# Weights requested ahead of K and V and used two heads later, a first MLP layer in single-column steps, and the last dx sums moved to the end

## The chip, the cores and the metric

The kernel runs on one core of a Trainium2 chip. The metric is the device time of one execution in microseconds (us), median of several runs. TensorE is called PE, VectorE DVE, ScalarE ACT, GpSimd POOL and SyncE SP. In this kernel SP issues all loads, in program order, and POOL issues all large stores.

## The reference, cut to what matters

One decoding step of a gated mix of attention and an MLP, forward and backward. There are 32 heads; each has a K and a V cache of 4096 x 128 in bf16 (1 MiB each), which must be read once, and gradients dK and dV of the same size, which must be written once.

```python
def _A_ref(x, k_cache, v_cache, wq, wo):          # x: [1, 1, 640]
    q = (x @ wq).reshape(B, Sq, H, Dh).transpose(0, 2, 1, 3)
    scores = jnp.einsum("bhqd,bhkd->bhqk", q, k_cache) * (Dh ** -0.5)
    p = _softmax(scores, axis=-1)
    o = jnp.einsum("bhqk,bhkd->bhqd", p, v_cache)
    return o.transpose(0, 2, 1, 3).reshape(B, Sq, H * Dh) @ wo
def _B_ref(x, w1, b1, w2):                        # F = 1728
    h = x @ w1 + b1
    return (h * tanh(softplus(h))) @ w2
# out = g * a + (1 - g) * b;  g = sigmoid(sum(x * gate_w))
# returned: out, and the gradients of x, k_cache, v_cache, wq, wo, w1, b1, w2, gate_w
```

K, V, wq, wo, w1 and w2 are 82 MB to read; their gradients are 82 MB to write. The arithmetic is that of one query row, so the work is a copy with some matrix-vector products on the way.

## The kernel before

Heads come in groups of four. One pass of `period(h)` handles a head: transposes of V on PE, softmax, dP, dV, dQ, and, for head h+1, the transposes of K and the scores. K and V of head h+3 are requested when head h starts (four buffers each). A group needs weights: a wo tile (640 KB, three buffers) and half of a wq tile (1280 KB, two buffers).

```python
def load_k(h):                                   # load_v, load_wq, load_wo and load_w2 alike, all on SP
    if h < H:
        kts[h] = kv_in.tile([P, J, Dh], BF16, name="Kn", tag="Kn", bufs=KB)   # KB = 4
        nc.sync.dma_start(kts[h][:], Kv[h])
```

Everything that is not a head's own work is cut into steps. A step has a kind (P for PE, D for DVE, T for a trifle) and names the steps that must be done in an earlier slot. `slot` is called three times in a head; it runs what is ready, up to p steps of kind P and d of kind D.

```python
def slot(h, p=2, d=1):
    slot_no[0] += 1
    room = {"P": p, "D": d, "T": 99}
    for kind in ("T", "D", "P"):
        for st in list(steps):
            name, k, fn, deps, head = st
            if k != kind or head > h or not room[k]:
                continue
            if all(done.get(x, 1 << 30) < slot_no[0] for x in deps):
                fn(); done[name] = slot_no[0]; steps.remove(st); room[k] -= 1
```

`prep_steps(g)` prepares a group: `qcol` (20 matmuls of x with wq), `doa` and `dob` (DVE sums over wo), and broadcasts of both. `finish_steps(g)` makes dwo in place of wo and stores it, and, for a whole wq tile, five dx sums. `mlp_steps()` is the MLP:

```python
def h_part(a, b):                                # first layer, columns a to b of 18
    def f():
        hps["t"] = gr_ps.tile([FP, FCN], F32, name="h_ps", tag="gr")
        for fc in range(a, b):
            for rc in range(RC):                 # RC = 5 matmuls a column
                nc.tensor.matmul(hps["t"][:, fc:fc + 1],
                                 lhsT=w1_sb[:, rc, :].rearrange("p (q c) -> p q c", c=FCN)[:, :, fc],
                                 rhs=x_bf[:, rc:rc + 1], start=(rc == 0), stop=(rc == RC - 1))
    return f
# ...
for k in range(0, FCN, 3):
    add(f"h{k}", "P", h_part(k, k + 3), (f"hadd{k - 3}",) if k else (), H0)
    add(f"hadd{k}", "T", h_add(k, k + 3), (f"h{k}",), H0)
# ... w2 comes in three chunks with two buffers: b{c} and dh{c}_{i} read chunk c,
#     dw2 overwrites it and stores it, and then chunk 2 is loaded into the buffer of chunk 0
        if c < 2:
            done[f"w2_{c}"] = -1
        else:
            add(f"w2_{c}", "T", lambda c=c: load_w2(c), (f"dw2_{c - 2}",), H0)
```

The loop over the heads and the end:

```python
for h in range(H):
    hh, g = h % G, h // G
    load_k(h + 3)
    load_v(h + 3)
    if hh == 0 and g + 1 < NG:                   # preparation of the next group goes first in the list
        rest = steps[:]; steps.clear(); prep_steps(g + 1, h); steps.extend(rest)
    if hh == 3:
        load_wo(g + 2)                           # (asserts cut)
        if g % 2 == 0:
            load_wq(g // 2 + 1)
    # ... (dwq blocks from head H - 3 on, cut)
    period(h)
    # ... (finish_steps(g) after the fourth head, cut)
dk_half(H - 1, 0); dk_half(H - 1, 1)
while steps:
    slot(H, 9, 9)                                # among these the five dx sums of the last wq tile
dwq_l = wts.tile([P, RC, GD], BF16, name="dwq_l", tag="wo_g", bufs=3)
for rc in range(RC):
    nc.vector.tensor_scalar(dwq_l[:, rc, :], dq_bc[:, CL:], x_f[:, rc:rc + 1], None, ALU.mult)
nc.gpsimd.dma_start(dwq_v[:, :, CL:], dwq_l[:])
# ... (out, dx and dgate_w from small columns: three small stores)
```

## Time and profile before

| | before |
|---|---|
| time, median of 3 runs | 441.23 us (440.04 to 445.35) |
| span of the profiled execution | 440.2 us |
| moved by DMA | 165.06 MB, mean 375 GB/s |
| PE, DVE, ACT busy | 71%, 70%, 40% |

The first lines are from the profile's page of the kernel before. The rows of section 2 cut the span into 40 slices of 11 us: PEclk is the granted clock in tenths, DMA the busy share of the 16 DMA engines in tenths, GB/s what they moved.

```profile
span 440.2 us, 15621 instructions
...
PE 314.6 (71%) x6932; PEld 291.8 (66%) x6932; DVE 306.6 (70%) x782; ACT 174.8 (40%) x394; POOL 50.6 (11%) x92
...
PEclk9999688596899999879995899959989899999755
DMA  7999999986899999989999799999999999997994
GB/s 251 422 391 399 424 426 414 381 329 214 348 387 362 400 393 389 416 323 391 375 420 409 276 363 400 422 388 360 324 415 422 418 381 422 421 406 305 407 417 187
DMA packets 26336, 165.06 MB, mean 375 GB/s; under 512 B 2812, under 2 KB 2812, under 8 KB 10012
```

No engine is full, while many slices stand at 414 to 426 GB/s and others far below. At 422 GB/s the 165.06 MB take 391 us. This gives a useful measure: *lost capacity*. A window of 10 us at 234 GB/s has lost 10 x (422 - 234) / 422 = 4.5 us, and 391 us plus all such losses is the span.

The next lines are from the chain of waits of the kernel before (start, length, what): the chain of work that ended last, in order of time.

```profile
54.00 28.07 DMA wq_g<-in_A_wq_dram
82.11 0.69 PE qc_ps L258 x20
...
164.34 23.19 DMA wq_g<-in_A_wq_dram
...
215.21 24.09 DMA wo_g<-in_A_wo_dram
```

The `qcol` step of a group, and the DVE sums, wait for weights that were requested just before, behind two more MB of K and V. The windows of the kernel before show what such a wait does. The columns are stretch, length, busy us (and instructions) of PE, PEld, DVE, ACT and POOL, granted clock, DMA share, GB/s.

```profile
90.00:100.00 10.00, 9.06 (x172) 8.51 (x170) 6.25 (x17) 4.79 (x10) 0.53 (x1) 1.00 0.76 306
100.00:110.00 10.00, 9.35 (x134) 9.12 (x135) 4.26 (x12) 2.83 (x8) 1.07 (x2) 0.66 0.68 234
...
230.00:240.00 10.00, 0.00 (x0) 0.00 (x0) 0.68 (x1) 0.00 (x1) 0.00 (x0) 0.55 1.01 423
240.00:250.00 10.00, 8.28 (x156) 7.87 (x157) 9.45 (x25) 4.74 (x11) 0.53 (x1) 0.77 0.68 251
```

From 230 to 240 us PE did nothing and DMA was full, because it was still prefetching. The damage comes afterwards: the K and V buffers are full and no dK or dV is ready to be stored, so from 240 to 250 us DMA moves 251 GB/s. From 90 to 110 us there is a second pattern: PE is busy and yet DMA is starved. There the blocks of 15 first-layer matmuls lie, and the clock falls during some of them, not all (1.00 from 90 to 100 us). These are half-microsecond windows of the first such block, in the same columns:

```profile
45.00:45.50 0.50, 0.50 (x6) 0.50 (x4) 0.43 (x3) 0.00 (x0) 0.00 (x0) 1.00 1.12 475
47.00:47.50 0.50, 0.50 (x4) 0.50 (x5) 0.00 (x0) 0.00 (x0) 0.00 (x0) 0.50 1.01 426
```

Last, four waits of the kernel before (engine, line, what it waited for: us in total, times, longest): those of PE and DVE for weights, and two of SP's own. The first of SP's holds K and V back while a chunk of w2 waits for its buffer to be stored.

```profile
PE qc_ps L258 <- DMA wq_g<-in_A_wq_dram: 27.1, 4, 11.0
DVE junk L268 <- DMA wo_g<-in_A_wo_dram: 28.5, 6, 11.4
...
SPq L138 <- DMA out_dram<-w2c: 11.5, 1, 11.5
SPq L132 <- DMA out_dram<-wo_g: 3.4, 2, 2.5
```

### The profile page before, as it was taken

Reading aid. Unit: us, or ns where it says so; the run is one execution under the profiler, and the core shown is the slowest. Engines: PE = TensorE matmul, PEld = TensorE weight load, DVE = VectorE, ACT = ScalarE, POOL = GpSimd, SP = SyncE. Lnnn points to the kernel's source line nnn. Section 1 sums busy time; section 2 is a strip of 40 time slices with the busy share of each in tenths; the row PEclk is TensorE's granted clock in tenths of the full one; section 3 lists DMA queues with packets and bytes.
Section 4 is the critical chain, followed back from the end, with each engine's and each line's share of the span. In section 5 each row is a group of like instructions: output and inputs, shape, how many; then the busy total and the mean of one; then the engine's idle time right before and its main releaser. Section 6 shows DMA issues by size and latency. Waiting matters only on the chain.

```text
span 440.2 us, 15621 instructions
## 1 busy us (share of the span) xinstructions
PE 314.6 (71%) x6932; PEld 291.8 (66%) x6932; DVE 306.6 (70%) x782; ACT 174.8 (40%) x394; POOL 50.6 (11%) x92
## 2 busy tenths in 40 slices
PE   2688997598978788298870988439885988888310
PEld 2687997588877687187770878438784877778200
DVE  3385353544489888468962999447975999999980
ACT  2365242243345445154540555215643545546100
POOL 0001000000000100002100011000200011112520
PEclk9999688596899999879995899959989899999755
DMA  7999999986899999989999799999999999997994
GB/s 251 422 391 399 424 426 414 381 329 214 348 387 362 400 393 389 416 323 391 375 420 409 276 363 400 422 388 360 324 415 422 418 381 422 421 406 305 407 417 187
DMA packets 26336, 165.06 MB, mean 375 GB/s; under 512 B 2812, under 2 KB 2812, under 8 KB 10012
## 3 DMA queue, kind: packets, MB, share of 16 engines
q1 hardware_dynamic: 14156, 82.03, 48.1%
q0 software_dynamic: 12112, 82.03, 45.4%
q8 instruction: 54, 0.88, 0.8%
q14 instruction: 14, 0.11, 0.1%
HBM read 82.03 MB, written 82.03 MB: 373 GB/s over the span
## 4 chain that ended last, share of the span: by engine, by line
PE 28%; DVE 27%; DMA 25%; issue 10%; ACT 6%; POOL 1%; SPq 1%; ACTq 0%; POOLq 0%; DVEq 0%
DMA wq_g<-in_A_wq_dram 12%; DMA wo_g<-in_A_wo_dram 11%; PE tr L527 10%; DVE dK_sb L549 7%; ACT tT L529 6%; DVE dV_sb L549 5%; PE sA L535 4%; PE sB L646 4%; PE sA L593 3%; DVE junk L354 3%; DMA out_dram<-wo_g 3%; PE h_ps L383 2%; DVE junk L268 2%; DVE junk L484 1%; DVE dwq_t L665 1%
## 5 line engine op out<-in xcount | busy, mean ns | idle before, releaser
L529 ACT COPY tT<-tr 128x512 f32<-128x512 f32 x256 | 143.3, 588 | 170.1 <-PE tr L527 169.8
L535 PEld LDWEIGHTS <-tT 128*128 128x128 bf16 x2048 | 77.1, 98 | 39.7 <-ACT tT L529 29.9
L527 PE MATMUL tr<-ident_bf,Kn 128*128 128x128 bf16 x1024 | 84.9, 239 | 2.3 <-issue 2.3
L549 DVE TENSOR_TENSOR dV_sb<-p_bf,qd 128x2048 bf16<-128x2048 bf16 x64 | 78.0, 1219 | 0.2 <-issue 0.2
L549 DVE TENSOR_TENSOR dK_sb<-ds_bf,qd 128x2048 bf16<-128x2048 bf16 x64 | 77.7, 1216 | 0.0
L527 PE MATMUL tr<-ident_bf,Vn 128*128 128x128 bf16 x1024 | 74.7, 225 | 0.1
L527 PEld LDWEIGHTS <-Kn 128*128 128x128 bf16 x1024 | 72.0, 109 | 3.4 <-issue 2.7
L535 PE MATMUL sA<-qdc,tT 128*128 128x48 bf16 x1024 | 50.8, 190 | 26.2 <-ACT dq_all L651 15.2
L527 PEld LDWEIGHTS <-Vn 128*128 128x128 bf16 x1024 | 64.3, 101 | 0.7 <-issue 0.2
L268 DVE SCALAR_TENSOR_TENSOR junk<-wo_g,da_bc 128x640 bf16<-128x640 bf16 x32 | 26.3, 822 | 29.1 <-DMA wo_g<-in_A_wo_dram 28.5
L535 PE MATMUL sB<-qdc,tT 128*128 128x48 bf16 x1024 | 46.2, 183 | 0.0
L576 POOL DMA_DIRECT2D out_dram<-dV_sb x32 | 17.7, 553 | 196.2 <-DVE dV_sb L549 162.3
L646 PE MATMUL sB<-ds_bf,Kn 128*128 128x48 bf16 x1024 | 34.5, 189 | 3.3 <-issue 1.9
L593 PEld LDWEIGHTS <-Vn 128*128 128x128 bf16 x1024 | 30.5, 96 | 8.8 <-issue 8.5
L566 POOL DMA_DIRECT2D out_dram<-dK_sb x31 | 18.0, 580 | 153.5 <-DVE rz L615 73.9
L593 PE MATMUL sA<-e_bf,Vn 128*128 128x48 bf16 x1024 | 31.5, 183 | 5.6 <-DVE zs L613 1.6
L646 PEld LDWEIGHTS <-Kn 128*128 128x128 bf16 x1024 | 31.4, 100 | 3.8 <-issue 3.7
L597 DVE TENSOR_REDUCE m<-sA 128x1 f32<-128x32 f32 x32 | 6.1, 190 | 36.2 <-PE sA L535 36.1
L627 PE MATMUL sB<-ident_f,part 128*128 128x128 f32 x32 | 10.8, 339 | 19.8 <-DVE pj L624 19.6
L258 PE MATMUL qc_ps<-cols_bf,wq_g 128*128 128x1 bf16 x160 | 5.3, 165 | 27.1 <-DMA wq_g<-in_A_wq_dram 27.1
L354 DVE SCALAR_TENSOR_TENSOR junk<-wq_g,dq_bc 128x1024 bf16<-128x1024 bf16 x20 | 24.3, 1217 | 0.1
L633 DVE TENSOR_SCALAR_CACHE_REDUCE dj<-sB,rz 128x128 f32<-128x128 f32 x32 | 11.1, 346 | 18.6 <-PE sB L627 18.6
(137 smaller groups left out, 294.9 us busy)
## 6 DMA issues: line engine op xcount, KB each, us to landing
Kn<-in_A_k_cache_dram SPq DMA_DIRECT2D x32, 1024.0 KB, 8.6
Vn<-in_A_v_cache_dram SPq DMA_DIRECT2D x32, 1024.0 KB, 16.9
out_dram<-dV_sb POOLq DMA_DIRECT2D x32, 1024.0 KB, 9.2
out_dram<-dK_sb POOLq DMA_DIRECT2D x31, 1024.0 KB, 10.3
wq_g<-in_A_wq_dram SPq DMA_DIRECT2D x4, 1280.0 KB, 6.7
wo_g<-in_A_wo_dram SPq DMA_DIRECT2D x8, 640.0 KB, 16.5
out_dram<-wo_g POOLq DMA_DIRECT2D x8, 640.0 KB, 9.3
out_dram<-dwq_t POOLq DMA_DIRECT2D x5, 896.0 KB, 11.9
```

Of the source, the lines that this page charges most:

```text
L268: nc.vector.scalar_tensor_tensor(junk[:, 0:D], in0=wos[g][:, i, :], scalar=1.0, in1=da_bc[:], op0=ALU.mult, op1=ALU.mult, accum_out=gp["do ...
L354: nc.vector.scalar_tensor_tensor(junk[:], in0=wqs[w][:, rc, :], scalar=1.0, in1=dq_bc[:, w * WG * Dh:(w + 1) * WG * Dh], op0=ALU.mult, op1 ...
L527: nc.tensor.transpose(tp[:, t, :], src[:, c * 8 + t, :], ident_bf[:])
L529: nc.scalar.copy(f32v(sb[:].rearrange("p a b -> p (a b)")), f32v(tp[:].rearrange("p a b -> p (a b)")))
L535: nc.tensor.matmul(out[:, j:j + W], lhsT=tb[:, t, :], rhs=vec.to_broadcast([P, W]), start=True, stop=True)
L549: nc.vector.tensor_tensor(dst[:, a:b, :].rearrange("p j (a b) -> p j a b", b=2), col[:, a:b, :].unsqueeze(2).to_broadcast([P, n, Dh // 2, 2]),
L566: nc.gpsimd.dma_start(dKv[h], st["dK"][:])
L576: nc.gpsimd.dma_start(dVv[h], st["dV"][:])
L593: nc.tensor.matmul(O, lhsT=vts[h][:, j, :], rhs=st["e"][:, j:j + 1].to_broadcast([P, W]), start=(j == 0), stop=(j == J - 1))
L627: nc.tensor.transpose(PT, part[:].to_broadcast([P, P]), ident_f[:])
L633: nc.vector.tensor_scalar(dj[:], PT, rz[:], None, ALU.mult, ALU.add, accum_out=dd[:])
L646: nc.tensor.matmul(DQ, lhsT=kts[h][:, j, :], rhs=ds[:, j, 0:1].to_broadcast([P, W]), start=(j == 0), stop=(j == J - 1))
```

## The change

Its intent: let no head wait for weights, break up the long PE blocks, keep SP from waiting for the w2 store, and let the last large store leave before the last sums. The diff, with context cut:

```diff
         def h_part(a, b):
             def f():
-                hps["t"] = gr_ps.tile([FP, FCN], F32, name="h_ps", tag="gr")
+                hps[a] = gr_ps.tile([FP, FCN], F32, name="h_ps", tag="gr")
# ... (hps["t"] becomes hps[a] in h_part and h_add)
-        for k in range(0, FCN, 3):
-            add(f"h{k}", "P", h_part(k, k + 3), (f"hadd{k - 3}",) if k else (), H0)
-            add(f"hadd{k}", "T", h_add(k, k + 3), (f"h{k}",), H0)
-        add("act1", "D", act1, (f"hadd{FCN - 3}",), H0)
+        for k in range(FCN):
+            add(f"h{k}", "P", h_part(k, k + 1), (f"hadd{k - 2}",) if k > 1 else (), H0)
+            add(f"hadd{k}", "T", h_add(k, k + 1), (f"h{k}",), H0)
+        add("act1", "D", act1, (f"hadd{FCN - 1}",), H0)
# ...
-                add(f"w2_{c}", "T", lambda c=c: load_w2(c), (f"dw2_{c - 2}",), H0)
+                for k in range(4):
+                    add(f"w2w{k}_{c}", "T", lambda: None, (f"w2w{k - 1}_{c}" if k else f"dw2_{c - 2}",), H0)
+                add(f"w2_{c}", "T", lambda c=c: load_w2(c), (f"w2w3_{c}",), H0)
# ... (the last slot of a head)
-        slot(h)
+        slot(h, 2, 2)
# ... (the loop over heads; asserts cut)
+        if hh == 3:
+            load_wo(g + 2)
+            if g % 2 == 0:
+                load_wq(g // 2 + 1)
         load_k(h + 3)
         load_v(h + 3)
-        if hh == 0 and g + 1 < NG:
+        if hh == 1 and g + 1 < NG:
# ...
-        if hh == 3:
-            load_wo(g + 2)
-            if g % 2 == 0:
-                load_wq(g // 2 + 1)
# ... (the end)
+    last = [st for st in steps if st[0].startswith("dx")]
+    steps[:] = [st for st in steps if not st[0].startswith("dx")]
     while steps:
         slot(H, 9, 9)
# ... (dwq_l is made and stored)
+    steps.extend(last)
+    while steps:
+        slot(H, 9, 9)
```

More of the change, by code (lines that the diff above doesn't have):

```diff
@@ L379, in f @@
             def f():
-                hps["t"] = gr_ps.tile([FP, FCN], F32, name="h_ps", tag="gr")
+                hps[a] = gr_ps.tile([FP, FCN], F32, name="h_ps", tag="gr")
                 for fc in range(a, b):
                     for rc in range(RC):
-                        nc.tensor.matmul(hps["t"][:, fc:fc + 1],
+                        nc.tensor.matmul(hps[a][:, fc:fc + 1],
                                          lhsT=w1_sb[:, rc, :].rearrange("p (q c) -> p q c", c=FCN)[:, :, fc],
@@ L392, in f @@
                     m["h"] = T("h_sb")
-                nc.vector.tensor_tensor(m["h"][:, a:b], hps["t"][:, a:b], b1f[:, a:b], ALU.add)
+                nc.vector.tensor_tensor(m["h"][:, a:b], hps[a][:, a:b], b1f[:, a:b], ALU.add)
             return f
@@ L682 @@
         hh, g = h % G, h // G
+        if hh == 3:
+            assert g == 0 or f"dwo{g - 1}" in done
+            load_wo(g + 2)
+            if g % 2 == 0:
+                assert g == 0 or f"dx{RC - 1}_{g - 1}" in done
+                load_wq(g // 2 + 1)
         load_k(h + 3)
         load_v(h + 3)
-        if hh == 0 and g + 1 < NG:
+        if hh == 1 and g + 1 < NG:
             rest = steps[:]
@@ L689 @@
             steps.extend(rest)
-        if hh == 3:
-            assert g == 0 or f"dwo{g - 1}" in done
-            load_wo(g + 2)
-            if g % 2 == 0:
-                assert g == 0 or f"dx{RC - 1}_{g - 1}" in done or True
-                assert g == 0 or f"dx{g - 1}{RC - 1}_" in done or f"dx{RC - 1}_{g - 1}" in done
-                load_wq(g // 2 + 1)
         if h == H - 3:
```

## The prediction

> **What bounds it now.** The page: 165.06 MB of DMA in a 440.2 us span, 375 GB/s. In 10 us windows, undisturbed ones hold 418 to 427 GB/s (the Trainium skill, "Perfetto Trace Analysis", Roofline, gives a lone core's 16 engines about 435). At 422 the bytes alone need 391 us (my estimate). PE (71%) and DVE (70%) are not full; where nothing stalls, heads pass every 9.3 to 9.4 us (K load issues: 355.9, 365.3, 374.6), under the 12.2 us that a head's share of the bytes needs. So DMA should bound it; the 49 us above 391 are lost DMA capacity. From the windows: 4.5 us in the ramp, 6 in the tail, 38 between: about 10.5 from 80 to 120 us, 5 from 120 to 170, 5 from 190 to 220, 6 from 240 to 270, 5 from 290 to 320, 5 from 350 to 410.
>
> **Why it is lost.** (a) At a group's first head the matmuls for q, or the sums of do, wait for weights requested just before, behind that head's K and V. The chain of waits shows wq 28.1 us (54 to 82), 23.2 (164 to 188), wo 24.1 (215 to 239), 16.9 (322 to 339). PE idles some 8 to 12 us each time. DMA stays full then, prefetching, but afterwards no stores are ready and it sinks: 167 GB/s at 240-245, 274 at 190-195. (b) The MLP's first layer runs in blocks of 15 matmuls, 2.7 to 2.9 us; the granted clock falls to 0.50 during or after them for 3 to 7 us (46.5 to 53.5, 101 to 108). Heads 3 to 6 take 14 to 19 us. The skill ("TensorE: Matmul & The Clock Gate", Part 1) has the clock follow PE activity over windows of about 3.4 us; these spells fit. (c) SP waits 11.5 us for a w2c store, holding back K and V.
>
> **What the change does.** Weights go ahead of K and V and are used about two heads (20 us or more) later: (a) should vanish; K and V come up to 1.9 MB, 5 to 9 us, later, with two heads of them buffered. First-layer blocks become 5 matmuls, about 0.9 us, one per slot over heads 2 to 8; the clock should hold. The w2c reload waits four more slots, freeing SP; but its dh product comes one slot after the request, so DVE should stall there (head 15) some 5 to 10 us: a draw. A fourth DVE step per head ends the MLP at head 26, not 30. The last dx sums (5 x 1.24 us) move behind the last dwq store; DMA is full until 433 anyway: 0 to 1 us.
>
> **On the critical path:** the 38 us between ramp and tail; I expect 29 back: (a) 19, (b) 7, last heads 3. 391 + 4.5 + 6 + 9 = about 411 us.
>
> **What would show it.** PE's and DVE's waits on wq and wo (about 28 us each) fall under 5; mean DMA rate 400 or more; no 10 us window between 20 and 390 us under 340, except near head 15; clock near 1.0 from 85 to 120 us; waits for K and V instead. Wrong if the rate falls to 350 with full queues, SP waits for dwo stores ahead of K and V, or head 15's stall is large.
>
> Predicted 411 us, 8 in 10 between 403 and 425; faster by over 2% 0.93, within 2% 0.06, slower 0.01.

## The result, and the profile after

| | before | after |
|---|---|---|
| time, median | 442.40 us (4 runs, 440.04 to 445.35) | 423.93 us (4 runs, 423.37 to 425.10) |
| ratio | | 0.9583, 95% interval 0.9517 to 0.9649 |
| span of the profiled execution | 440.2 us | 423.3 us |
| mean DMA rate | 375 GB/s | 390 GB/s |

A ratio here is the mean time of one kernel's runs over that of the other's of the same rounds, so it is not quite the ratio of the medians quoted. The change made the kernel 4.2% faster. The measured time lies inside the predicted range, near its upper end, 13 us above the predicted middle.

The page of the changed kernel (slices are now 10.6 us):

```profile
span 423.3 us, 15629 instructions
...
PEclk9999899999998999798855899999999899979855
DMA  7999999999999999999983799999999999999991
GB/s 243 424 411 395 422 423 417 424 420 426 422 423 422 423 415 423 422 423 422 414 312 147 292 343 392 412 421 423 420 424 422 424 422 420 424 407 399 411 409 59
```

The row of GB/s has become flat at about 422, with one hole of five slices in the middle. The windows of the changed kernel, columns as before:

```profile
90.00:100.00 10.00, 9.29 (x199) 8.75 (x199) 5.71 (x18) 4.26 (x9) 1.07 (x2) 1.00 1.02 423
100.00:110.00 10.00, 9.09 (x174) 8.61 (x172) 6.47 (x17) 4.91 (x11) 1.06 (x2) 1.00 1.01 422
...
210.00:220.00 10.00, 0.00 (x0) 0.00 (x0) 0.00 (x0) 0.00 (x0) 0.00 (x0) 0.50 0.97 349
220.00:230.00 10.00, 4.15 (x68) 4.03 (x69) 4.66 (x11) 1.71 (x4) 0.54 (x1) 0.50 0.30 122
230.00:240.00 10.00, 9.19 (x193) 8.70 (x190) 8.79 (x23) 3.98 (x9) 0.53 (x1) 0.73 0.67 256
240.00:250.00 10.00, 8.33 (x225) 7.69 (x222) 9.82 (x26) 5.73 (x14) 1.59 (x3) 1.00 0.91 341
```

From 90 to 110 us the clock stays at 1.00 and DMA is full. From 210 to 220 us no engine works at all, and then DMA sinks to 122 GB/s, lower than in any such window of the kernel before. The waits of the changed kernel name the cause:

```profile
DVE junk L449 <- DMA w2c<-in_B_w_dram: 20.3, 1, 20.3
...
PE qc_ps L258 <- DMA wq_g<-in_A_wq_dram: 3.7, 2, 2.8
DVE junk L268 <- DMA wo_g<-in_A_wo_dram: 3.7, 1, 3.7
...
SPq L132 <- DMA out_dram<-wo_g: 59.7, 5, 16.7
```

PE's wait on wq went from 27.1 us to 3.7, DVE's on wo from 28.5 to 3.7. In their place stands a single wait of 20.3 us: line 449 is the dh product of the reloaded w2 chunk. Its timeline in the changed kernel (start, length, engine and line; in brackets the idle time before and what ended it):

```profile
193.62 0.33 SPq L117 DMA_DIRECT2D Kn<-in_A_k_cache_dram  x1
194.00 0.44 SPq L122 DMA_DIRECT2D Vn<-in_A_v_cache_dram  x1
194.57 0.40 SPq L138 DMA_DIRECT2D w2c<-in_B_w_dram  x1
...
202.70 1.86 DVE L458 TENSOR_SCALAR w2c<-db_bc,act_f 96x640 bf16<-96x640 bf16 x6
224.81 0.88 DVE L449 SCALAR_TENSOR_TENSOR junk<-w2c,dm,db_bc 96x640 bf16<-96x640 bf16 x1 [20.25 <-DMA w2c<-in_B_w_dram]
```

The chunk is requested at 194.6 us, right behind a K and a V, because the four empty steps put the request into head 15. Its first reader stands in DVE's queue one slot later and holds the engine from 204.6 to 224.8 us. Landing took 30.2 us. For most of that time DMA moved some 380 to 430 GB/s, but in the last 9 us much less, though the chunk was not yet whole (windows of the changed kernel):

```profile
216.00:218.00 2.00, 0.00 (x0) 0.00 (x0) 0.00 (x0) 0.00 (x0) 0.00 (x0) 0.50 1.02 264
222.00:224.00 2.00, 0.00 (x0) 0.00 (x0) 0.00 (x0) 0.00 (x0) 0.00 (x0) 0.50 0.51 187
```

The packet records of the kept trace add that the chunk is 96 packets (six for each of the 16 DMA engines, if shared evenly) and that its last six, one after another, end 4.4 us after the other 90 were done (5.8 us in experiment 4, 6.6 in experiment 1). So one engine that is late, as at the end of the kernel (experiments 11 and 12), seems to have lengthened the wait; no run here tests that.

That loads in general land later in the changed kernel is shown by the DMA issues; the first line is of the kernel before, the others of the changed one (the last number is the median time from issue to landing in us):

```profile
Kn<-in_A_k_cache_dram SPq DMA_DIRECT2D x32, 1024.0 KB, 8.6
...
Kn<-in_A_k_cache_dram SPq DMA_DIRECT2D x32, 1024.0 KB, 20.4
Vn<-in_A_v_cache_dram SPq DMA_DIRECT2D x32, 1024.0 KB, 27.1
```

The span, in lost capacity (10 us windows at 422 GB/s): 391 + 4.4 to 20 us + 1.0 from 20 to 200 us + 16.2 from 200 to 270 us + 0 from 270 to 380 us + 10.6 from 380 us to the end = 423.

### The profile page after: what moved, and what is told of

Its sections match the earlier page's. It is cut to its first block, busy times and chain, and to the rows that moved or that the text cites. A ratio compares the mean times of both kernels' runs of the same rounds, so it can differ in the third digit from the quotient of the medians.

```text
span 423.3 us, 15629 instructions
## 1 busy us (share of the span) xinstructions
PE 306.7 (72%) x6932; PEld 283.4 (67%) x6932; DVE 307.4 (73%) x794; ACT 174.5 (41%) x394; POOL 50.9 (12%) x92
## 3 DMA queue, kind: packets, MB, share of 16 engines
q1 hardware_dynamic: 14156, 82.03, 47.6%
## 4 chain that ended last, share of the span: by engine, by line
DVE 32%; DMA 31%; PE 24%; ACT 7%; issue 3%; SPq 1%; ACTq 0%; DVEq 0%
DMA Kn<-in_A_k_cache_dram 13%; PE tr L529 8%; DVE dK_sb L551 8%; DMA w2c<-in_B_w_dram 7%; DVE dV_sb L551 7%; DMA out_dram<-dK_sb 7%; ACT tT L531 6%; DVE junk L354 4%; DMA Vn<-in_A_v_cache_dram 4%; PE sB L648 3%; PE h_ps L383 3%; PE sA L537 3%; PE sA L595 3%; DVE junk L484 2%; DVE junk L268 2%
## 5 line engine op out<-in xcount | busy, mean ns | idle before, releaser
L529 PE MATMUL tr<-ident_bf,Kn 128*128 128x128 bf16 x1024 | 80.5, 232 | 6.2 <-DMA Kn<-in_A_k_cache_dram 5.1
L529 PEld LDWEIGHTS <-Kn 128*128 128x128 bf16 x1024 | 67.7, 105 | 7.2 <-DMA Kn<-in_A_k_cache_dram 5.4
L537 PE MATMUL sA<-qdc,tT 128*128 128x48 bf16 x1024 | 49.1, 187 | 23.2 <-ACT dq_all L653 16.4
L568 POOL DMA_DIRECT2D out_dram<-dK_sb x31 | 19.0, 613 | 169.3 <-DVE rz L617 86.5
L648 PE MATMUL sB<-ds_bf,Kn 128*128 128x48 bf16 x1024 | 32.1, 185 | 9.7 <-DVE ds_bf L637 8.3
L648 PEld LDWEIGHTS <-Kn 128*128 128x128 bf16 x1024 | 29.3, 97 | 10.1 <-issue 10.1
L449 DVE SCALAR_TENSOR_TENSOR junk<-w2c,dm,db_bc 96x640 bf16<-96x640 bf16 x18 | 15.7, 874 | 20.5 <-DMA w2c<-in_B_w_dram 20.3
L603 PE MATMUL sA<-ident_f,m 128*128 128x128 f32 x32 | 9.6, 301 | 24.8 <-DVE m L599 24.8
L603 PEld LDWEIGHTS sA<-ident_f,m 128*128 128x128 f32 x32 | 4.5, 140 | 26.4 <-DVE m L599 26.2
## 6 DMA issues: line engine op xcount, KB each, us to landing
Kn<-in_A_k_cache_dram SPq DMA_DIRECT2D x32, 1024.0 KB, 20.4
Vn<-in_A_v_cache_dram SPq DMA_DIRECT2D x32, 1024.0 KB, 27.1
```

The costliest lines, as they stand in the source:

```text
L449: nc.vector.scalar_tensor_tensor(junk[0:FP, 0:D], in0=w2cs[c][:, i, :], scalar=m["dm"][:, fc:fc + 1], in1=db_bc[0:FP, :], op0=ALU.mult, op ...
L529: nc.tensor.transpose(tp[:, t, :], src[:, c * 8 + t, :], ident_bf[:])
L537: nc.tensor.matmul(out[:, j:j + W], lhsT=tb[:, t, :], rhs=vec.to_broadcast([P, W]), start=True, stop=True)
L568: nc.gpsimd.dma_start(dKv[h], st["dK"][:])
L603: nc.tensor.transpose(MM, m32[:].to_broadcast([P, P]), ident_f[:])
L648: nc.tensor.matmul(DQ, lhsT=kts[h][:, j, :], rhs=ds[:, j, 0:1].to_broadcast([P, W]), start=(j == 0), stop=(j == J - 1))
```

## The experiments

Twelve runs were made of eleven kernels (experiment 1 was run twice), in four calls. Those ran beside the kernel before. All were of the fast state and all but the last gave the right result. Across calls only ratios to the kernel before are compared.

### 1. The reloaded chunk is used later

The changed kernel, but the readers of the reloaded chunk wait for six more empty steps. The best kernel; the others below are built on it.

```diff
-            add(f"b{c}", "P", b_part(c), ("act2",) + ...
+            add(f"b{c}", "P", b_part(c), ("act2", f"w2u5_{c}") + ...
-                add(f"dh{c}_{i}", "D", dh_part(c, i), ("act2", f"w2_{c}"), H0)
+                add(f"dh{c}_{i}", "D", dh_part(c, i), ("act2", f"w2u5_{c}"), H0)
# after the step w2_{c}; done[f"w2u5_{c}"] = -1 for the chunks 0 and 1
+                for k in range(6):
+                    add(f"w2u{k}_{c}", "T", lambda: None, (f"w2u{k - 1}_{c}" if k else f"w2_{c}",), H0)
```

> The changed kernel, but the products that read the reloaded w2 chunk come six slots (about two heads) after its request, not one. Theory A (one stall of 20.3 us at that reload cost the changed kernel about 16 us of DMA capacity, 210 to 260 us): DVE's wait for w2c falls under 2 us, no 10 us window between 20 and 390 us falls under 380 GB/s, time 408 to 412 us. Rival B (SP's 59.7 us of waiting for dwo stores, ahead of K and V, holds the loads back): w2c's wait goes, but the time stays at 419 or more, and K and V waits grow by as much.

Measured: 415.15 us (415.02 to 415.74), ratio 0.9381 (0.934 to 0.9422). DVE no longer waits for w2c at all and PE's wait for it is 2.6 us; no window between 20 and 390 us is under 387 GB/s. Where the changed kernel had its hole, DMA is now full (same columns, experiment 1):

```profile
210.00:220.00 10.00, 7.03 (x175) 6.20 (x172) 9.82 (x25) 3.92 (x10) 0.53 (x1) 1.00 1.02 418
220.00:230.00 10.00, 6.62 (x129) 6.35 (x130) 6.02 (x16) 2.75 (x8) 1.06 (x2) 0.68 1.01 425
```

SP still waits 60.7 us for dwo stores, as long as in the changed kernel, and PE now waits 12.7 us for wq. So theory A stands: the hole was made by one wait, and SP's waiting for stores, which the prediction had named as a danger, can have cost no more than the 4.8 us that are still lost in the middle. The time is 3 us above the range that A expected. In lost capacity the span of 413.4 us is 391 + 4.4 + 4.8 from 20 to 380 us + 12.9 from 380 us to the end: the middle lost 12.5 us less than in the changed kernel, but the end 2.3 us more. Experiments 11 and 12 are about that end.

### 2. and 3. One part of the change alone

Experiment 2 is the kernel before with only the loop's part of the diff (weights ahead of K and V, preparation at the second head). Experiment 3 is the kernel before with only the single-column steps. Their edits are those hunks of the diff above.

> The kernel before with only the move of the wo and wq requests ahead of K and V and of the next group's preparation to the second head. The prediction gave this part 19 us: then 422 to 425 us, and the windows at 190, 240 and 300 us no longer sink under 340 GB/s, while those from 90 to 120 us still do (blocks of 15 first-layer matmuls). If the first-layer blocks matter little once the weights come early, 410 to 416 us; if the blocks are most of it, 430 or more.

Measured: 422.85 us (420.13 to 423.09), ratio 0.9539 (0.9488 to 0.9589). The windows at 190, 240 and 300 us are at 392, 422 and 414 GB/s, those from 90 to 120 us at 293, 311 and 328. This is the predicted picture and the predicted size. One part alone does as much as the whole change, because the whole change also brought the stall at w2c: here SP waits 13.7 us for the store, the reload is requested at 176.7 us and first read at 207.7 us, and no DVE wait for w2c appears.

> The kernel before with only the single-column steps of the first layer. Prediction: 7 us, so 434 to 436 us, the granted clock near 1.0 between 85 and 120 us apart from the stretch just after the wait for wq. Rival: the stalls on weights come at the same places and swallow it, 438 to 442 us.

Measured: 436.02 us (435.75 to 437.24), ratio 0.9858 (0.9805 to 0.9912), 6 us: clear of the noise. Time as predicted; the clock only in part, since waits for wq are still there (33.4 us on PE) and cool PE as well: 1.00, 0.83 and 0.72 in the windows from 90 to 120 us.

### 4. Without the four empty steps

```diff
-                for k in range(4):
-                    add(f"w2w{k}_{c}", "T", lambda: None, ...)
-                add(f"w2_{c}", "T", lambda c=c: load_w2(c), (f"w2w3_{c}",), H0)
+                add(f"w2_{c}", "T", lambda c=c: load_w2(c), (f"dw2_{c - 2}",), H0)
```

> The changed kernel without the four empty steps ahead of the w2 reload: the request goes out as soon as the second half of dw2 is done, so it stands in SP's queue ahead of the K and V that it followed, and SP waits for the w2c store. Theory A: SP waits up to 12 us there, but the chunk is in time or nearly (DVE's wait for it under 6 us), 410 to 415 us: the four steps caused the stall that they were meant to spare. Rival: SP's wait costs what it cost in the kernel before, and the time stays at 420 to 426 us.

Measured: 417.29 us (415.92 to 417.45), ratio 0.942 (0.9377 to 0.9464). SP waits 11.7 us for the store, as expected; DVE's wait for the chunk is 12.1 us, twice what theory A allowed, and the time lies between the two ranges. The direction is clear: of the changed kernel's 20.3 us of stall the empty steps made 8, and taking them away gains 1.7% (0.942 against 0.9583). They spared SP a wait that cost little and gave DVE one that cost much. They did not even make the request later: with SP's wait it goes out at 194.2 us here and at 194.6 us in the changed kernel, but here ahead of that head's K and V, there behind them.

### 5., 7. and 8. One part taken out of experiment 1

A second run of experiment 1 stood beside these three.

> The same kernel as e1_w2_use_late, to stand beside the three that each take one part out of it on this chip: 414 to 416.5 us, the same by every theory.

Measured: 416.29 us (415.94 to 416.81), ratio 0.9404 (0.9355 to 0.9454).

Experiment 5 has the blocks of 15 matmuls again (the first two hunks of the diff undone).

> e1_w2_use_late with the first layer again in blocks of 15 matmuls. Theory (the blocks hold PE up and let its clock fall, heads 3 to 6 become longer than their share of the DMA's work): 420 to 423 us, windows between 85 and 120 us under 340 GB/s. Rival (once weights never stall PE, the heads have slack enough): 417 or less, no such windows.

Measured: 424.06 us (422.57 to 425.86), ratio 0.9582 (0.9527 to 0.9637), 7.8 us over its reference, more than expected. The starved windows are back (same columns, experiment 5):

```profile
90.00:100.00 10.00, 9.04 (x169) 8.84 (x168) 7.30 (x24) 3.42 (x9) 1.07 (x2) 0.84 0.76 315
100.00:110.00 10.00, 8.15 (x180) 7.61 (x176) 6.74 (x21) 4.33 (x12) 1.06 (x2) 0.86 0.78 269
```

Experiments 3 and 5 show what the blocks cost. They do not separate the fall of the clock from the blocks' own time on PE: both go with the same edit, and the first layer's work is also spread out by it (its last matmul starts at 99.3 us in experiment 5, at 118.0 us in its reference).

Experiment 7 requests the weights behind K and V again, but still uses them two heads later; experiment 8 keeps the request ahead and uses them one head later.

```diff
# experiment 7
+        load_k(h + 3)
+        load_v(h + 3)
         if hh == 3:
             load_wo(g + 2)
             if g % 2 == 0:
                 load_wq(g // 2 + 1)
-        load_k(h + 3)
-        load_v(h + 3)
# experiment 8
-        if hh == 1 and g + 1 < NG:
+        if hh == 0 and g + 1 < NG:
```

> e1_w2_use_late with wo and wq requested behind K and V again, but still used two heads later. If the later use is what matters: 413 to 418 us, and PE's and DVE's waits on wq and wo stay under 6 us together. If the place in the queue matters: 420 or more, with waits on wq and wo of 10 us or more.

> e1_w2_use_late with the weights still ahead of K and V, but used one head after the request as in the kernel before (the first layer's steps then come up to two in a slot). A full DMA lands them some 18 to 20 us after the request (the changed kernel's profile), one head is 10 to 12 us, so PE and DVE should wait 5 to 10 us in each of six groups: 418 to 428 us. If the place in the queue alone cures it, 414 to 417 us.

Measured: experiment 7 418.65 us (418.39 to 419.47), ratio 0.9461 (0.9419 to 0.9503); experiment 8 421.12 us (420.44 to 422.65), ratio 0.9525 (0.9473 to 0.9578). So the loss of one half costs 2.4 us or 4.8 us against the reference, where the whole move was worth 19 us in experiment 2: either half alone keeps most of the gain. (In experiment 7 the runs lie apart from the reference's, but the intervals of the ratios overlap.) Experiment 8 came out as expected. Experiment 7 fits neither of its theories: the time is near the first, the waits are those of the second. They are:

```profile
PE qc_ps L258 <- DMA wq_g<-in_A_wq_dram: 24.7, 3, 17.1
...
DVE junk L268 <- DMA wo_g<-in_A_wo_dram: 10.5, 3, 5.4
...
SPq L132 <- DMA out_dram<-wo_g: 11.7, 2, 10.8
```

Here is a lesson that I had not expected. Experiment 7 waits 35 us for weights, two thirds of the kernel before's 56, yet it is only 2.4 us slower than its reference, which itself waits 18 us (14.4 for wq, 3.9 for wo). And SP's waits for dwo stores fell from 58 to 12 us without a gain that shows. A wait, even a long one, costs only what DMA capacity is lost after it; here the queue was mostly deep enough. (In experiment 8 up to two first-layer columns fall into one slot, so part of its 4.8 us may be that.)

### 6. and 9. The end of the kernel

Experiment 6 is experiment 1 with the last hunk of the diff undone (dx sums before the last dwq store). Experiment 9 is experiment 1 with `slot(h)` in place of `slot(h, 2, 2)`.

> e1_w2_use_late with the last dx sums ahead of the last dwq store again, as in the kernel before. If the end is set by DMA's backlog (prediction: 0 to 1 us for this part): 0.934 to 0.944 of the kernel before, like e1's 0.938 and 0.940, with the last store landing within 1 us of e1's. If the order mattered, the last store leaves POOL 6 us later and the time grows by 3 to 6 us: 0.948 or more.

> e1_w2_use_late with one DVE step, not two, in a head's last slot, as in the kernel before: the MLP's DVE work then runs on to head 31, and the five dwq blocks are made only after the last head. Prediction gave the fourth step about 3 us at the end; by the trace the five blocks (1.1 us each) and the stores behind them come late, so 4 to 9 us slower than e1: 0.947 to 0.962 of the kernel before. If the DMA's backlog covers it, within 2 us of e1.

Measured: experiment 6 415.73 us (414.72 to 416.43), ratio 0.9412 (0.9355 to 0.9469); experiment 9 416.30 us (415.16 to 418.30), ratio 0.9433 (0.938 to 0.9486). Both lie within the interval of experiment 1's second run (0.9355 to 0.9454), on another chip. The order of the last sums is worth nothing measurable, as predicted. My first expectation for experiment 9 was wrong, its alternative (within 2 us) right: DMA is at 248 GB/s from 370 to 380 us and 342 in the next window, while the dwq blocks come only from 384 us on; then it is at 407, and the loss is balanced by a shorter end (8.1 us lost from 390 us on, 12.9 in experiment 1).

### 11. and 12. What the end consists of

In experiment 1 DMA does not stop at once. Windows of its last microseconds (columns as before; the DMA share is the last number but one):

```profile
398.00:400.00 2.00, 0.45 (x1) 0.18 (x1) 1.23 (x11) 0.00 (x0) 0.00 (x0) 0.50 0.94 388
402.00:404.00 2.00, 0.00 (x0) 0.00 (x0) 0.00 (x0) 0.00 (x0) 0.00 (x0) 0.50 0.07 28
406.00:408.00 2.00, 0.00 (x0) 0.00 (x0) 0.00 (x0) 0.00 (x0) 0.00 (x0) 0.50 0.07 28
```

A share of 0.07 of 16 engines is one engine, working at 28 GB/s for some 7 us while the other 15 have finished. In the kernel before there is no such stretch:

```profile
432.00:434.00 2.00, 0.00 (x0) 0.00 (x0) 0.00 (x0) 0.00 (x0) 0.00 (x0) 0.50 0.93 384
434.00:436.00 2.00, 0.00 (x0) 0.00 (x0) 0.00 (x0) 0.00 (x0) 0.00 (x0) 0.50 0.23 88
```

Experiment 11 takes work from the engine of the highest number:

```diff
-            nc.sync.dma_start(vts[h][:], Vv[h])
+            if h % 8 == 3:
+                nc.sync.dma_start(vts[h][0:120], Vv[h][0:120])
+                nc.sync.dma_start(vts[h][120:128], Vv[h][120:128])
+            else:
+                nc.sync.dma_start(vts[h][:], Vv[h])
```

> e1_w2_use_late with four of the 32 V loads split into 120 and 8 partitions. In e1's trace one DMA engine of the 16 works on alone for 8 us after the others are done. The Trainium skill (DMA: Bandwidth & Descriptors, Latency and other measured facts) says that engines 7 and 15 are usually the slower ones, and (Why a DMA increments its semaphore by 16) that a 120-partition transfer uses the lowest 15 engines, one of 8 partitions the lowest 8. If engine 15 is the slow one, it is relieved of four times 64 KB, 2.5 us each at the 309 ns that 8 KB take: the lonely tail shrinks from 8 us to under 2 and the time falls by 4 to 7 us, to 408 to 412. If another engine is slow, the tail stays 8 us or grows and the time stays at 414 to 418.

Measured: 419.43 us (418.95 to 421.09), ratio 0.9506 (0.9456 to 0.9556), and one engine again alone for about 7 us. So, if the cited rule for the choice of engines holds here, it is not engine 15; the trace does not number the engines, so no run here shows the rule. The kernel with the split loads is 1% slower than experiment 1; why was not looked into.

Experiment 12 takes PE's instructions away (results wrong):

```diff
-        o_part(0, J)
+        o_part(0, 1)
-        for j in range(J):                       # the DQ matmuls
+        for j in (0, J - 1):
```

> e1_w2_use_late with 1 of the 32 O matmuls and 2 of the 32 DQ matmuls per head (wrong results on purpose): PE gets 9896 instructions instead of 13800, all loads and stores stay. The Trainium skill (Runtime: NRT & Kernel Launch, Instruction fetch mechanics) has instructions fetched in blocks of 256 over the sequencer's own DMA queue; the profile's instruction queue q8 moved 54 packets of 16 KB, and 13800 / 256 is 53.9. Theory (the DMA engine that works on alone at the end is the one that also fetches PE's instructions): q8 falls to about 39 packets, 15 fewer, some 9 us less work for that engine at the rate of the others (309 ns for 8 KB), the lonely tail of 6 to 8 us shrinks under 3 us and the time to 407 to 411 us, 0.921 to 0.931 of the kernel before. Rival (that engine is slow for another cause): q8 falls as well, but the tail stays 6 us or more and the time 413 to 417 us.

Measured: 409.81 us (409.58 to 410.40), ratio 0.9272 (0.9221 to 0.9323). The instruction queue in experiment 12 fell from 54 packets to 39, as expected:

```profile
q8 instruction: 39, 0.64, 0.6%
```

But one engine is again alone, from 397 to 403 us. The time is in the theory's range and the tail is in the rival's, so the theory falls: the time fell for another reason. In lost capacity, the windows from 20 to 390 us of experiment 12 lost 1.4 us where those of experiment 1 lost 4.9, so most of the 5 us came from a PE with less work, which leaves fewer holes in the DMA's work. Why one engine lags stays open. What can be said is when. One engine is alone for 5.5 to 8 us where DMA was full almost from the start to the end (experiments 1, 2, 4, 6, 7, 11 and 12), about 4 us in the changed kernel, whose queue ran dry at 220 us, 2.5 us in experiment 9, with its hole at 370 us, and under 2 us in the kernel before and in experiment 3, whose queues ran dry between 390 and 410 us. This fits a lag that adds up while the queue is full, about 2% of the time, and is caught up in a hole: in the changed kernel's hole, too, the DMA share stands at 0.06 to 0.08, one engine, from 225 to 229 us. That it is always the same engine is not shown.

## Why the prediction was right, and where its size was off

1. *What bounds it: DMA capacity lost after stalls.* Right. The windows in which DMA was full stayed mostly at 415 to 428 GB/s in every run, and the losses go where the waits go (experiments 1, 2 and 5). That 391 us and all losses add up to the span is arithmetic, and proves nothing.
2. *Part (a), weights: 19 us.* Right: 0.9539, which is 19.0 us by the medians, alone (experiment 2). That it fits to the tenth is luck, as that kernel's runs spread over 3 us. Either half of the move alone keeps most of it (7 and 8).
3. *Part (b), blocks and clock: 7 us.* Right: 5.9 us alone by the medians (experiment 3), 7.8 us when taken out (experiment 5). The two parts add up: experiment 1, which has both and no stall, has 0.9381, and 0.9539 x 0.9858 is 0.940. That the clock is what the blocks cost was argued, not shown.
4. *"DVE should stall there (head 15) some 5 to 10 us: a draw."* This is the step that was mis-sized. The place and the mechanism were right; the stall was 20.3 us, and the windows from 200 to 270 us lost 16.2 us. Taking the stall out was worth 2.1% (0.9381 against 0.9583). What was too small is the time that the chunk needs to land: DVE was ready for it 10 us after the request, so a stall of 5 to 10 us meant a landing within 15 to 20 us; it took 30.2. The kernel before could not show this term. There the same reload is requested at 206.6 us and first read at 269.8 us, 63 us later, since six reads of the chunk before it (203 to 223 us) and that chunk's dw2 (to 266.8 us) come first, at one DVE step a slot. In the changed kernel the first read comes 10 us behind the request, and loads land later (K 20.4 us, not 8.6).
5. *"4.5 + 6" for ramp and tail.* The ramp was 4.4. The end was the second term that was too small: from the last full window on, the changed kernel lost 9.1 us (410 to 423.3 us) where the kernel before had lost 6.1 (430 to 440.2 us). About 4 us of it is the one DMA engine that finishes after the others. Together: 391 + 4.5 + 6 + 9 was predicted; with the same cut at 410 us the middle lost 18.7 instead of 9, the end 9.1 instead of 6, which makes the 13 us.
6. *Last heads, 3 us; dx order, 0 to 1 us.* The first was not there (experiment 9, within the noise of experiment 1); the second was as said (experiment 6).
7. *Signs.* Waits on wq and wo under 5 us each: 3.7 and 3.7. Clock near 1.0 from 85 to 120 us: yes. No window under 340 GB/s but near head 15: yes (349, 122, 256 and 341 from 210 us on). Mean rate 400 or more: no, 390; experiment 1, without the stall, has 399. Waits for K instead: yes, but small (5.1 us on PE). "SP waits for dwo stores ahead of K and V" was named as a danger and came true (59.7 us), but experiment 1 has as much of it and loses no more than 4.8 us in the middle.

The best correct version is experiment 1: 415.15 us, 6.2% faster than the kernel before (6.0% in its second run) and 2.1% faster than the changed one.

## What to carry to other kernels

When DMA is the limit, count lost capacity, not waits: a wait is paid only where the transfer engines run dry after it. When a change fills the DMA queue, expect every other load to land later than in the old profile, and move the readers of late requests by that much. When a change moves steps, count again how long before its first reader each load is requested: here 63 us became 10 us. A fix for one wait (empty steps that spare SP) should be tried with and without once the rest has changed, as its cost moves too.

## What the Trainium skill lacked or had wrong

- "TensorE: Matmul & The Clock Gate", Part 1, ties the clock to how busy PE is. In the kernel before, PE's row was busy without a gap from 111.6 to 115.0 us (3.40 of 3.40 us, 32 matmuls, 15 of them of one column), and at 115.0 us the granted clock fell to 0.50 all the same. A row that shows PE busy does not mean that the clock holds; the page has no word on how matmuls of one column count, and no run here shows it. With 5 instead of 15 in a row the clock stayed at 1.00 from 80 to 120 us; it still fell from 47.6 to 51.0 us, around a wait of PE.
- "DMA: Bandwidth & Descriptors", Latency and other measured facts, gives latencies and names slower engines, but neither how long a load takes to land behind a full queue (median for K 8.6 us before, 20.4 us after; 30.2 us for the w2 chunk) nor by how much one engine falls behind (5.5 to 8 us in 400 us of full queue). Of the two engines that it names, 7 and 15, experiment 11 speaks against 15, as far as the page's own rule for the choice of engines holds.
- "Perfetto Trace Analysis", Roofline, gives about 435 GB/s as the bound of a lone core's 16 engines. Full 10 us windows mostly held 415 to 428 GB/s here, and the engine that finishes last costs up to 8 us more at the end.
